# Attention with mixed heads, then a feed-forward block: a fixed order of TensorE's pieces, one ring of eight PSUM banks, and a shorter set-up

## The chip, the cores and the metric

The kernel runs on one core of one Trainium2 chip. The metric is the device time of one execution in microseconds (us); several executions give a median. "Span" is the time from the first to the last instruction in the profiled execution, some 1.7 us less than that execution's time. Engines are named as in the profile: PE is TensorE's matmuls, PEld its weight loads, DVE is VectorE, ACT is ScalarE, POOL is GpSimd.

## The reference, cut to what matters

Eight batches, twelve heads, 448 positions, head size 64. The scores of all heads are mixed by a 12x12 matrix before the softmax, the probabilities are mixed by another 12x12 matrix after it, and the result goes through a feed-forward block with a squared ReLU.

```python
scores = scale * q @ k.T                              # (8, 12, 448, 448)
scores = einsum('bhij,hg->bgij', scores, w_pre)       # mix the heads
attn = softmax(scores)
attn = einsum('bhij,hg->bgij', attn, w_post)          # mix the heads again
x = (attn @ v)  as (3584, 768)
h = maximum(x @ w_in, 0)                              # 768 -> 2048
out = (h * h) @ w_out                                 # 2048 -> 768
```

## The kernel before

A batch is worked through in 14 chunks of 32 query rows. For a chunk, TensorE makes three score tiles (`s_ps`: four 32-column matmuls each), three mixed tiles (`m_ps`), and, after the softmax, four tiles of the post product (`at_ps`), which come out transposed. Three chunks are in flight: scores of chunk s, mix of s-1, post product of s-2. The value product (`ot_ps`), the feed-forward block (`h_ps`, `o_ps`) and the transposes of the next batch's queries and keys (`qt_ps`, `kt_ps`) are "filler": units with a nominal weight, taken from a list after each step. A scheduler that works when the kernel is built settles the order on each engine, with program order as priority.

```python
psS = ... tile_pool(name="psS", bufs=2, space=PSUM)      # scores
psM = ... tile_pool(name="psM", bufs=2, space=PSUM)      # mixes
psT = ... tile_pool(name="psT", bufs=2, space=PSUM)      # post products
psF = ... tile_pool(name="psF", bufs=2, space=PSUM)      # filler
...
def ot_unit(b, half, c2):                                # value product of two heads
    for hh in range(2):                                  # one head after the other
        for jb in range(3):
            matmul(ps[64*hh:64*hh+64, 0:SH], lhsT=vfull[x][jb][:, g, :], rhs=at[:, jb, g, :], ...)
        for u in range(2):
            matmul(ps[64*hh:64*hh+64, ...], lhsT=vlast[x][u][:, g, :], rhs=at3[:, g, :], ...)
...
def chunk_mix(b, c):                                     # third mixed tile: two 64-column pieces
    matmul(ps[:, 0:S], lhsT=preBB, rhs=Bt, start=True, ...)
    for u, A in enumerate((A0, A1)):
        matmul(ps[64*u:64*u+64, 0:S], lhsT=preA[:, 128:192], rhs=A, ...)
...
for s in range(len(steps) + 2):
    chunk_scores(s); chunk_mix(s - 1); chunk_post(s - 2)
    ...                                                  # put new filler on the list
    debt = run_filler(3200 + debt)
```

The softmax here doesn't subtract the row's maximum and nothing guards it: scores larger than these inputs give would overflow.

Of the kernel before, what the change touches and what calls it, by code (L numbers as in the profile page):

```python
# [8 lines left out]
BF16 = mybir.dt.bfloat16  # L9
F32 = mybir.dt.float32  # L10
ACT = mybir.ActivationFunctionType
ALU = mybir.AluOpType

B, H, S, D = 8, 12, 448, 64
DMODEL = H * D
# [20 lines left out]
def kernel(  # L36
# [20 lines left out]
    psS = ctx.enter_context(tc.tile_pool(name="psS", bufs=2, space=bass.MemoryType.PSUM))  # L57
    psM = ctx.enter_context(tc.tile_pool(name="psM", bufs=2, space=bass.MemoryType.PSUM))
    psT = ctx.enter_context(tc.tile_pool(name="psT", bufs=2, space=bass.MemoryType.PSUM))
    psF = ctx.enter_context(tc.tile_pool(name="psF", bufs=2, space=bass.MemoryType.PSUM))  # L60
# [5 lines left out]

    def load_qk(b):
        qs, ks = [], []
        for st in range(4):
            n = ROWS[st]  # L70
            rows = slice(128 * st, 128 * st + n)
            qst = stage.tile([P, H, D], BF16, name="qst", tag="qst", bufs=4)
            nc.gpsimd.dma_start(out=qst[0:n, :, :], in_=q[b, :, rows, :].rearrange("h s d -> s h d"))  # L73
            qs.append(qst)
            kst = stage.tile([P, H, D], BF16, name="kst", tag="kst", bufs=4)
            nc.gpsimd.dma_start(out=kst[0:n, :, :], in_=k[b, :, rows, :].rearrange("h s d -> s h d"))
            ks.append(kst)
        return qs, ks
# [10 lines left out]
    staged = {0: load_qk(0)}  # L89


    ident = consts.tile([P, P], BF16, name="ident")
    masks.make_identity(nc, ident[:, :])
    onescol = consts.tile([P, 1], BF16, name="onescol")
    nc.vector.memset(onescol[:, :], 1.0)
    onesblk = consts.tile([P, 64], BF16, name="onesblk")
    nc.vector.memset(onesblk[:, :], 1.0)

    istripe = consts.tile([P, HC], F32, name="istripe")
    nc.vector.tensor_copy(out=istripe[:, :], in_=ident[:, 0:16])  # L100
    for r in range(1, 8):
        nc.vector.tensor_add(out=istripe[:, :], in0=istripe[:, :], in1=ident[:, 16 * r:16 * r + 16])

    def wcol(w, name, heads):
        t = consts.tile([P, H], F32, name=name)
        for j, h in enumerate(heads):
            src = bass.AP(tensor=w.tensor, offset=w[h, 0:1].offset, ap=[[0, HC], [1, H]])
            eng = nc.sync if j % 2 == 0 else nc.scalar
            eng.dma_start(out=t[HC * j:HC * j + HC, 0:H], in_=src)
        return t  # L110

    HA, HB = list(range(8)), [8, 9, 10, 11, 8, 9, 10, 11]

    def cat(w, name, heads):
        col = wcol(w, name + "_col", heads)
        t = consts.tile([P, H * HC], BF16, name=name)
        for g in range(H):
            nc.vector.tensor_scalar_mul(out=t[:, g * HC:(g + 1) * HC], in0=istripe[:, :], scalar1=col[:, g:g + 1])
        return t

    preA = cat(w_pre, "preA", HA)
    preB = cat(w_pre, "preB", HB)

# [8 lines left out]

    ql = []
    for x in range(2):
        ql.append([])
        for p in range(NPAIR):
            t = consts.tile([P, NHC, 32], BF16, name=f"ql{x}_{p}")
            nc.gpsimd.memset(t[:, :, :].rearrange("p a b -> p (a b)"), 0.0)
            ql[x].append(t)
    for x in range(2):  # L140
        for u in range(2):
            nc.gpsimd.memset(vlast[x][u][64 - 64 * u:128 - 64 * u, :, :].rearrange("p a b -> p (a b)"), 0.0)

    postA = cat(w_post, "postA", HA)
    postB = cat(w_post, "postB", HB)
# [5 lines left out]

    wpost_bf = consts.tile([H, H], BF16, name="wpost_bf")
    nc.gpsimd.dma_start(out=wpost_bf[:, :], in_=w_post[0:H, 0:H])
    cg_ps = psF.tile([P, 512], F32, name="cg_ps", tag="psF")
    nc.tensor.matmul(cg_ps[0:64, 0:H], lhsT=onesblk[0:H, 0:64], rhs=wpost_bf[0:H, 0:H], start=True, stop=True)
    nc.tensor.matmul(cg_ps[64:128, 0:H], lhsT=onesblk[0:H, 0:64], rhs=wpost_bf[0:H, 0:H], start=True, stop=True)
    cgblk = consts.tile([P, NPAIR], F32, name="cgblk")
    for hh in range(2):
        nc.vector.tensor_scalar_mul(
            out=cgblk[64 * hh:64 * hh + 64, :],  # L160
            in0=cg_ps[64 * hh:64 * hh + 64, 0:H].rearrange("p (c t) -> p t c", t=2)[:, hh, :],
            scalar1=1.0 / S)

    load_v(0)
    w1, w2 = [], []
    for c2 in range(NPAIR):
        t = wts.tile([P, DFF], BF16, name=f"w1_{c2}")
        nc.gpsimd.dma_start(out=t[:, :], in_=moe_w_in[c2 * 128:(c2 + 1) * 128, 0:DFF])
        w1.append(t)
    for ft in range(FT):  # L170
        t = wts.tile([P, DMODEL], BF16, name=f"w2_{ft}")
        nc.gpsimd.dma_start(out=t[:, :], in_=moe_w_out[ft * 128:(ft + 1) * 128, 0:DMODEL])
        w2.append(t)

    kts = {}
    bvecs = {}
    xts = {}
    h2ts = {}
    atbs = {}


    def prologue_units(b):
        qs, ks = staged[b]
        kts[b] = [None] * NPAIR

        def q_unit(p):
            ps = psF.tile([P, S], BF16, name="qt_ps", tag="psF")
            for st in range(4):
                n = ROWS[st]
                nc.tensor.transpose(ps[:, 128 * st:128 * st + n],  # L190
                                    qs[st][0:n, 2 * p:2 * p + 2, :].rearrange("s h d -> s (h d)"), ident[0:n, 0:n])
            for hh in range(2):
                r = slice(64 * hh, 64 * hh + 64)
                nc.vector.tensor_copy(out=ql[b % 2][p][r, :, 16 * hh:16 * hh + 16],
                                      in_=ps[r, 0:S].rearrange("p (n i) -> p n i", i=HC))

        def k_unit(p):
            ps = psF.tile([P, S], BF16, name="kt_ps", tag="psF")
            for st in range(4):
                n = ROWS[st]  # L200
                nc.tensor.transpose(ps[:, 128 * st:128 * st + n],
                                    ks[st][0:n, 2 * p:2 * p + 2, :].rearrange("s h d -> s (h d)"), ident[0:n, 0:n])
            kt_p = work.tile([P, S], BF16, name="kt_p", tag="kt", bufs=2 * NPAIR)
            nc.scalar.copy(out=kt_p[:, :], in_=ps[:, :])
            kts[b][p] = kt_p

        out_ = []
        for p in range(NPAIR):
            out_.append((300, lambda p=p: q_unit(p)))
            out_.append((300, lambda p=p: k_unit(p)))  # L210
        return out_

    def bias_unit(b):

        x = b % 2
        ps = psF.tile([P, 512], F32, name="vs_ps", tag="psF")
        srcs = vfull[x] + [vlast[x][0]]
        for c2 in range(NPAIR):
            for jb in range(4):
                nc.tensor.matmul(ps[:, c2:c2 + 1], lhsT=srcs[jb][:, 2 * c2:2 * c2 + 2, :].rearrange("s h d -> s (h d)"),  # L220
                                 rhs=onescol[:, 0:1], start=(jb == 0), stop=(jb == 3))
        bv = work.tile([P, NPAIR], F32, name="bvec", tag="bvec", bufs=2)
        nc.vector.tensor_tensor(out=bv[:, :], in0=ps[:, 0:NPAIR], in1=cgblk[:, :], op=ALU.mult)
        bvecs[b] = bv

    def ot_unit(b, half, c2):
        x = b % 2
        at, at3 = atbs[(b, half)]
        ps = psF.tile([P, 512], F32, name="ot_ps", tag="psF")
        for hh in range(2):  # L230
            g = 2 * c2 + hh
            r = slice(64 * hh, 64 * hh + 64)
            for jb in range(3):
                nc.tensor.matmul(ps[r, 0:SH], lhsT=vfull[x][jb][:, g, :], rhs=at[:, jb, g, :],  # L234
                                 start=(jb == 0), stop=False, skip_group_check=True)
            for u in range(2):
                nc.tensor.matmul(ps[r, 0:SH].rearrange("p (c u i) -> p u c i", u=2, i=HC)[:, u, :, :],  # L237
                                 lhsT=vlast[x][u][:, g, :], rhs=at3[:, g, :], start=False, stop=(u == 1),
                                 skip_group_check=True)
        if (b, c2) not in xts:  # L240
            xts[(b, c2)] = ffnp.tile([P, S], BF16, name="xt", tag=f"xt{c2}", bufs=2)
        nc.scalar.activation(out=xts[(b, c2)][:, SH * half:SH * half + SH], in_=ps[:, 0:SH], func=ACT.Identity,  # L242
                             bias=bvecs[b][:, c2:c2 + 1], scale=1.0)

    def ffn1_unit(b, ft):
        ps = psF.tile([P, S], F32, name="h_ps", tag="psF")
# [5 lines left out]
        nc.scalar.activation(out=hr[:, :], in_=ps[:, :], func=ACT.Relu)  # L252
# [182 lines left out]
```

## Time and profile before

| | before |
|---|---|
| time, median of 2 | 916.75 us (916.36 to 917.13) |
| span | 915.4 us |
| PE busy / ACT / DVE / POOL | 95% / 55% / 47% / 26% |
| changes of tile shape in TensorE's built order | 1306 |

The page of the kernel before begins with the busy time of each engine, its share of the span and its number of instructions:

```profile
span 915.4 us, 17324 instructions
PE 872.0 (95%) x6914; PEld 434.1 (47%) x6914; DVE 429.8 (47%) x1070; ACT 502.3 (55%) x1337; POOL 241.9 (26%) x277
```

PE is busy nearly all the time, so the other engines' idle time costs nothing. But a busy PE is not a streaming PE. Here is a piece of the timeline of PE before (start in us, duration in us, engine, line, operation, tiles; `128*32` is the part of the array used, rows times columns; the rest is shape and count):

```profile
312.88 0.35 PE L325 MATMUL m_ps<-s_sb,preBB 128*128 128x448 bf16 x1
313.16 0.38 PE L327 MATMUL m_ps<-s_sb,preA 128*64 128x448 bf16 x2
313.48 0.26 PE L353 MATMUL at_ps<-postA,d_sb 128*128 128x192 bf16 x1
...
313.89 0.25 PE L354 MATMUL at_ps<-postA,d_sb 128*128 128x192 bf16 x1
314.07 0.36 PE L300 MATMUL s_ps<-kt_p,ql_0_183 128*32 128x448 bf16 x1
...
314.08 0.36 PE L300 MATMUL s_ps<-kt_p,ql_3_189 128*32 128x448 bf16 x1
314.27 0.35 PE L300 MATMUL s_ps<-kt_p,ql_0_183 128*32 128x448 bf16 x1
```

A 448-column operand takes 187 ns to stream (448 columns at 2.4 per ns, the slope between 56 ns for 128 columns and 189 ns for 448 in this trace), and from 314.07 to 314.27, between two 32-column groups in the same shape, little more passes: 0.20 us. But from 312.88, a full-array matmul of 448 columns, to 313.16, where a 64-column pair starts, 280 ns pass; from there to the full-array matmul at 313.48 it is 320 ns; and a 192-column matmul, 80 ns of streaming, is followed by a narrow group only after 180 ns (313.89 to 314.07). Over the whole trace the medians after a 448-column matmul are 189 ns in the full array, 283 ns to narrow columns, 295 ns from 32 columns back to the full array and 309 ns from 64 columns back. A change of shape costs about 100 ns. The four `s_ps` quarters, on the other hand, start within 10 ns of each other (the first and the last are shown, at 314.07 and 314.08): narrow tiles of one shape run side by side.

The list of waits of PE before (who waited for whom; us in total, times, longest) shows that after the set-up it waits for nobody:

```profile
PE cg_ps L155 <- DVE preB L118: 23.8, 1, 23.8
PE kt_ps L201 <- DVE cgblk L159: 5.7, 1, 5.7
...
PE ot_ps L234 <- ACT xt L242: 0.9, 6, 0.2
```

The first two lines are the set-up. In the timeline of DVE it reads:

```profile
10.37 8.65 DVE L100 CAST istripe<-ident 128x16 f32<-128x16 bf16 x1 [8.97 <-POOL ident masks.py:199]
...
20.73 1.75 DVE L118 TENSOR_SCALAR preA<-istripe,preA_col 128x16 bf16<-128x16 f32 x12 [0.24 <-DVE istripe L102]
...
29.82 0.34 DVE L159 TENSOR_SCALAR cgblk<-cg_ps 64x6 f32<-64x6 f32 x2
30.19 0.79 DVE L194 COPY ql_0_183<-qt_ps 64x448 bf16<-64x448 bf16 x2
```

A small cast takes 8.65 us, then scalings in groups of twelve follow, and the first copy of queries (`ql`), without which no score can be made, starts at 30.19 us. The same trace shows what POOL does meanwhile, eleven memsets without a pause:

```profile
10.19 0.93 POOL L138 MEMSET ql_1_185<- 128x896 bf16 x1
...
18.05 0.93 POOL L138 MEMSET ql_5_205<- 128x896 bf16 x1
```

The last of them ends at 18.98 us, the cast at 19.02.

### The profile page before, as it was taken

The page shows a single profiled execution, that of the slowest core. Times are in us where ns is not written, and L with a number is a line of the kernel's source. Part 1 is how long each engine was busy: PE and PEld are TensorE (multiplying, and loading weights), DVE is VectorE, ACT ScalarE, POOL GpSimd, SP SyncE. Part 2 cuts the span into 40 slices and gives each one's busy share as a digit, 9 for nine tenths or more (in the row PEclk, how much of TensorE's full clock was granted, in tenths as well). Part 3 has the DMA queues.
Part 4 walks back from the last instruction along what each step waited for, and adds up shares of the span by engine and source line. Part 5 has one row for each costly group of instructions (what it writes and reads, how often), then busy time and mean ns, then how long its engine had stood idle before and what let it go on. Part 6 is the DMA issues. An engine that isn't in the chain of part 4 may idle for free. (4 is left out here: it accounts for less than half of the span.)

```text
span 915.4 us, 17324 instructions
## 1 busy us (share of the span) xinstructions
PE 872.0 (95%) x6914; PEld 434.1 (47%) x6914; DVE 429.8 (47%) x1070; ACT 502.3 (55%) x1337; POOL 241.9 (26%) x277
## 2 busy tenths in 40 slices
PE   0699999999999999999999999999999999999998
PEld 0234455453554545544454535545355444544354
DVE  5577730677017760277405772077701775036700
ACT  0266652677527764476635775267653676347641
POOL 9470343030700308003250215203070000600050
PEclk9999999999999999999999999999999999999999
DMA  9997951072510905109321275109051000010001
GB/s 61 178 189 41 62 35 44 19 48 15 35 62 1 62 1 44 53 1 62 26 36 37 18 45 35 52 11 59 4 35 62 1 2 1 16 47 1 2 1 61
DMA packets 149330, 35.76 MB, mean 39 GB/s; under 512 B 139264, under 2 KB 148480, under 8 KB 149248
## 3 DMA queue, kind: packets, MB, share of 16 engines
q0 software_dynamic: 140032, 23.60, 34.0%
q1 hardware_dynamic: 8704, 11.03, 3.5%
q8 instruction: 54, 0.88, 0.4%
q14 instruction: 28, 0.23, 0.1%
q10 hardware_dynamic: 512, 0.01, 0.0%
HBM read 47.21 MB, written 11.01 MB: 64 GB/s over the span
## 5 line engine op out<-in xcount | busy, mean ns | idle before, releaser
L357 DVE CAST at<-at_ps 128x384 bf16<-128x384 f32 x336 | 181.1, 550 | 394.0 <-PE at_ps L354 389.3
L312 ACT ACTIVATE e_sb<-m_ps 128x448 f32<-128x448 f32 x336 | 181.1, 542 | 51.3 <-ACT e_sb L312 18.7
L335 DVE TENSOR_SCALAR d_sb<-e_sb,rc 128x448 bf16<-128x448 f32 x336 | 137.1, 463 | 0.7
L304 ACT CAST s_sb<-s_ps 128x448 bf16<-128x448 f32 x224 | 115.8, 534 | 37.2 <-PE s_ps L300 36.5
L252 ACT ACTIVATE hr<-h_ps 128x448 f32<-128x448 f32 x128 | 69.5, 543 | 79.4 <-PE h_ps L248 72.8
L352 PE MATMUL at_ps<-postBB,d_sb 128*128 128x384 bf16 x336 | 111.0, 330 | 1.5 <-DVE d_sb L335 0.7
L73 POOL DMA_DIRECT2D qst<-in_q_dram x32 | 31.8, 993 | 275.7 <-PE qt_ps L190 223.9
L353 PE MATMUL at_ps<-postA,d_sb 128*128 128x192 bf16 x336 | 83.2, 248 | 0.0
L354 PE MATMUL at_ps<-postA,d_sb 128*128 128x192 bf16 x336 | 82.7, 246 | 0.0
L321 PE MATMUL m_ps<-s_sb,preA 128*128 128x448 bf16 x224 | 81.0, 362 | 0.0
L264 ACT COPY osb<-o_ps 128x384 f32<-128x384 f32 x48 | 23.0, 478 | 101.2 <-PE o_ps L262 101.2
L306 DVE CAST s_sb<-s_ps 128x448 bf16<-128x448 f32 x112 | 69.3, 618 | 8.7 <-PE s_ps L300 8.4
L312 ACT ACTIVATION_READ_ACCUMULATOR e_sb<-m_ps 128x1 f32 x336 | 66.8, 199 | 0.0
L242 ACT ACTIVATE xt<-ot_ps,bvec 128x224 bf16<-128x224 f32 x96 | 40.1, 447 | 23.3 <-PE ot_ps L237 23.1
L352 PEld LDWEIGHTS <-d_sb 128*128 128x128 bf16 x336 | 32.6, 97 | 40.2 <-issue 28.6
L248 PE MATMUL h_ps<-xt,w_0_272 128*128 128x448 bf16 x128 | 45.1, 352 | 1.2 <-ACT xt L242 0.5
L327 PE MATMUL m_ps<-s_sb,preA 128*64 128x448 bf16 x224 | 45.4, 378 | 0.0
L248 PE MATMUL h_ps<-xt,w_5_282 128*128 128x448 bf16 x128 | 45.1, 352 | 0.0
L248 PE MATMUL h_ps<-xt,w_4_280 128*128 128x448 bf16 x128 | 45.1, 352 | 0.0
L248 PE MATMUL h_ps<-xt,w_3_278 128*128 128x448 bf16 x128 | 45.1, 352 | 0.0
L248 PE MATMUL h_ps<-xt,w_2_276 128*128 128x448 bf16 x128 | 45.1, 352 | 0.0
L248 PE MATMUL h_ps<-xt,w_1_274 128*128 128x448 bf16 x128 | 45.1, 352 | 0.0
(862 smaller groups left out, 2097.1 us busy)
## 6 DMA issues: line engine op xcount, KB each, us to landing
out_dram<-osb SPq DMA_DIRECT2D x48, 192.0 KB, 1.9
qst<-in_q_dram POOLq DMA_DIRECT2D x24, 192.0 KB, 5.8
kst<-in_k_dram POOLq DMA_DIRECT2D x24, 192.0 KB, 6.3
out_dram<-osb SPq DMA_DIRECT2D x16, 96.0 KB, 2.2
qst<-in_q_dram POOLq DMA_DIRECT2D x8, 96.0 KB, 6.7
kst<-in_k_dram POOLq DMA_DIRECT2D x8, 96.0 KB, 6.5
v_0_85<-in_v_dram POOLq DMA_DIRECT2D x4, 192.0 KB, 4.0
v_1_86<-in_v_dram POOLq DMA_DIRECT2D x4, 192.0 KB, 5.0
```

Of the source, the lines that this page charges most:

```text
L248: nc.tensor.matmul(ps[:, 0:S], lhsT=w1[c2][:, ft * 128:(ft + 1) * 128], rhs=xts[(b, c2)][:, :], start=(c2 == 0), stop=(c2 == NPAIR - 1))
L252: nc.scalar.activation(out=hr[:, :], in_=ps[:, :], func=ACT.Relu)
L304: nc.scalar.copy(out=sb[:, :], in_=ps[:, :])
L306: nc.vector.tensor_copy(out=sb[:, :], in_=ps[:, :])
L312: nc.scalar.activation(out=e[:, :], in_=ps[:, :], func=ACT.Exp, scale=SCALE, accum_out=sm[:, t:t + 1])
L321: nc.tensor.matmul(ps[:, 0:S], lhsT=preA[:, 0:128], rhs=A[:, :], start=True, stop=False)
L327: nc.tensor.matmul(ps[64 * u:64 * u + 64, 0:S], lhsT=preA[:, 128:192], rhs=A[:, :], start=False, stop=True, skip_group_check=True)
L335: nc.vector.tensor_scalar(out=d[:, :], in0=es[t][:, :], scalar1=rc[:, t:t + 1], scalar2=1.0 / S, op0=ALU.mult, op1=ALU.subtract)
L352: nc.tensor.matmul(ps[:, 0:384], lhsT=dB[:, js], rhs=postBB[:, :], start=True, stop=False, skip_group_check=True)
L353: nc.tensor.matmul(ps[:, 0:192], lhsT=d0[:, js], rhs=postA[:, :], start=False, stop=True, skip_group_check=True)
L354: nc.tensor.matmul(ps[:, 192:384], lhsT=d1[:, js], rhs=postA[:, :], start=False, stop=True, skip_group_check=True)
L357: nc.vector.tensor_copy(out=dst, in_=src)
```

## The change

Its intent: take the narrow matmuls of a step together, so that TensorE changes its shape twice a step and not again and again; fix that order by hand; let all eight banks serve any tile; and shorten the set-up. The 64-column pieces become pairs of 32-column pieces, so that they have the scores' shape. The filler is spread evenly over the four places of each step. The diff, cut to its core:

```diff
-    psS, psM, psT, psF: four pools of two banks
+    psp = ctx.enter_context(tc.tile_pool(name="psp", bufs=8, space=bass.MemoryType.PSUM))
...
+    keys are loaded first, then queries; ql[0] is cleared on DVE, ql[1] and vlast on POOL later
-        for g in range(H):
-            nc.vector.tensor_scalar_mul(out=t[:, g * HC:(g + 1) * HC], in0=istripe[:, :], scalar1=col[:, g:g + 1])
+        nc.vector.tensor_tensor(out=t[:, :, :], in0=istripe (broadcast), in1=cols[name] (broadcast), op=ALU.mult)
...
+            for jb in range(3):              # value product: the heads alternate
+                for hh in range(2):
...
+    def mix_AB(s):                           # four 32-column pieces instead of two of 64
+        for r in range(4):
+            u, half = divmod(r, 2)
+            nc.tensor.matmul(ps[32 * r:32 * r + 32, 0:S], lhsT=preA[:, 128 + 32 * half:160 + 32 * half], ...)
...                                           # post_last: eight 32-column pieces instead of four of 64
+    with tc.manual_schedule(engines={PE}):
+            share = sum(w for w, _ in filler) / max(rest - 0.5, 1) / 4 if s0 else 1e9
+            score_tile(s0, 0); score_tile(s0, 1)
+            mix_AB(s1)
+            post_last(s2)
+            score_tile(s0, 2)
+            mix_BB(s1);     fill(share)
+            mix_O(s1, 0);   fill(share)
+            mix_O(s1, 1);   post(s2, 0);  fill(share)
+            post(s2, 1);    fill(share)
+            post(s2, 2)
```

(The `score_tile` to `post` lines stand for the body of the step loop, without its conditions.) The softmax's reciprocal is now taken for each tile alone, 336 of one column for 112 of three. The diff also joins the value product of two head pairs in one unit, cuts each output tile of the feed-forward block into two units, and starts the next batch's transposes two steps earlier.

## The prediction

> **What bounds the kernel now.** TensorE. On the page PE is busy 95% of the 915.4 us span, ACT 55%, DVE 47%, POOL 26%; in the list of waits PE hardly waits after start-up. But it isn't always streaming. In the timeline a 448-column matmul is followed by the next after 189 ns when both use the full array (448 columns at 2.4 per ns: 187). When the next has another tile shape, the step is 283 ns (128 to 32 or 64 columns), 295 (32 to 128) or 309 (64 to 128): about 100 ns per change of shape. This agrees with the Trainium skill, "TensorEngine Tiling (Array Packing)", Key Properties: changing the tiling mode drains TensorE.
>
> The built instruction order has 1306 such changes before, 540 after. Measured steps laid along the order (full array: columns/2.4; narrow tiles of one mode side by side; 98 ns per change) give 860 us for before. The real stream lags this sum by 24 us at its start, 40 us at 76 us, 51 us at the end: the sum is a usable ruler.
>
> **PE after.** The same ruler gives an estimate of 725 us: 135 less. 766 fewer changes are 75 us of it; the other 60 us are narrow matmuls that now run beside others of their group instead of alone (score quarters four together; the value product alternating two heads, 72 to 42 us). The 672 added narrow matmuls (four 32-column pieces for two of 64) cost no streaming time.
>
> **Other engines.** ACT stays at 502 us of work (64% of the new span), DVE at 430 plus some 20 for 224 more reciprocals. Neither is the limit on average. But per chunk ACT needs 2 x 0.53 + 3 x (0.54 + 0.20) + 0.32 = 3.6 us, PE without filler only 3.1. All 14 steps of batch 0 and the first two of each later batch have little filler, and in a fixed order PE waits there. At 4.3 us per such step this costs 13 us in batch 0 and 2.5 in each other: 30 together. Steps with filler take 6 to 8 us of PE, so waits for ACT and banks are mostly hidden; I allow 8 us.
>
> **Start-up.** Now steady PE work starts at 30 us, because DVE constants (one cast of 8.6 us, 48 scalings) precede the query copies. After: keys first, 4 wide multiplies for the 48; the last small weight load still lands near 15.5 us, so first scores at about 20 us. That is 15 us above the ruler, plus 4 for half-speed matmuls (0.55 us each instead of 0.36, seen until 51 us now).
>
> **Sum.** 725 + 15 + 4 + 30 + 8 + 5 (end) + 1.4 (span to time) = 789 us, 14% less; range 768 to 818.
>
> **What would show it.** The 100 ns steps remain at about 540 places; the value-product groups shrink; PE waits for ACT appear in the list of waits, in batch 0 and at batch starts; first scores near 20 us; PE about 95% busy elsewhere; ACT 64%.
>
> **What would make it wrong.** PE waiting in every step (softmax latency before the post product; banks of the one ring held by open accumulations): 0.3 us a step is 30 us. POOL memsets delaying DVE at the start. A cold clock through batch 0. Or thin steps costing nothing: 765.

## The result, and the profile after

| | before | after |
|---|---|---|
| time, median of 2 | 916.75 us | 792.89 us (792.84 to 792.94) |
| ratio | | 0.8649 (95%: 0.8612 to 0.8686) |
| span | 915.4 us | 791.2 us |
| PE / ACT / DVE busy | 95 / 55 / 47% | 95 / 61 / 62% |
| changes of shape in the built order | 1306 | 540 |
| laid-out stream (the prediction's ruler) | 859.9 us | 725.4 us |
| start of the last matmul less that stream ("lag") | 50.9 us | 61.2 us |
| first score matmul | 33.9 us | 22.6 us |

A ratio here is the mean time of one kernel's runs over that of the other's runs of the same rounds, so it is not quite the ratio of the medians quoted.

The page after, in the same lines as before:

```profile
span 791.2 us, 18851 instructions
PE 750.2 (95%) x7586; PEld 428.6 (54%) x7586; DVE 488.6 (62%) x1249; ACT 482.3 (61%) x1337; POOL 243.2 (31%) x271
```

The timeline of PE after shows the narrow group of one step: two score tiles, `mB_ps`, the last post product (L359, L363), the third score tile; then the full array until the next step:

```profile
205.64 0.36 PE L291 MATMUL s_ps<-kt_p,ql_0_143 128*32 128x448 bf16 x1
...
205.84 0.35 PE L291 MATMUL s_ps<-kt_p,ql_0_143 128*32 128x448 bf16 x1
...
206.03 0.36 PE L305 MATMUL mB_ps<-s_sb,preA 128*32 128x448 bf16 x4
206.22 0.25 PE L359 MATMUL at_ps<-postA,d_sb 128*32 128x192 bf16 x2
207.33 0.26 PE L359 MATMUL at_ps<-postA,d_sb 128*32 128x192 bf16 x2 [0.87 <-DVE d_sb L315]
207.34 0.34 PE L363 MATMUL at_ps<-postBB,d_sb 128*32 128x192 bf16 x4
...
207.51 0.35 PE L291 MATMUL s_ps<-kt_p,ql_5_148 128*32 128x448 bf16 x1
207.80 0.36 PE L321 MATMUL mB_ps<-s_sb,preBB 128*128 128x448 bf16 x1
208.00 0.35 PE L245 MATMUL h_ps<-xt,w_0_191 128*128 128x448 bf16 x1
```

Up to 206.22 everything is in one shape and the steps are those of streaming: 0.20, 0.19 and 0.19 us. From 207.51 to 207.80, where the shape changes, it is 0.29 us. In between there is a new thing: the last post product has started two of its matmuls at 206.22 and goes on only at 207.33; 0.87 us of this PE sat idle for the scaled softmax tile `d_sb`. The list of waits of PE after shows it in total:

```profile
PE at_ps L359 <- DVE d_sb L315: 20.3, 29, 3.4
PE kt_ps L180 <- DMA kst<-in_k_dram: 10.1, 4, 6.0
PE qt_ps L180 <- DMA qst<-in_q_dram: 3.6, 3, 1.5
PE kt_ps L180 <- DVE ql_0_143 L188: 0.7, 1, 0.7
```

20.3 us in 29 places. (This list counts only time in which no matmul at all is in flight; against the ruler the jumps at this place add to some 25 us between its own matmuls and 6 to 7 us just before it.) In this example the scaling for which PE waits took 1.13 us in place of the usual 0.45, beside a multiply of POOL's; experiment 11 returns to that.

The ruler and the trace together give a full account of the span, which can be set against the prediction's sum. The lag is read at the start of each step:

| term | predicted | read from the trace of after |
|---|---|---|
| stream | 725 | 725.4 |
| lag when the first score starts | 15 | 17.7 |
| half clock and waits in the 14 steps of batch 0 | 4 + 13 | 18.5 (some 4 in the first two steps, 5.4 in another) |
| waits in the other steps without filler | 17.5 | 16.3 (3.4 in batch 1, 2.1 in each of 6 more) |
| other waits | 8 | 8.7 |
| last matmul to end, span to time | 5 + 1.4 | 4.6 + 1.7 |
| sum | 789 | 792.9 |

The matmuls of 448 columns take 0.55 us each until 28.7 us, in the first two steps of batch 0. From 38.9 to 42.3 us, after TensorE's longest wait for `d_sb`, they take that long again, and there the profile shows a granted clock of 0.50; some 1.7 us of the step of 5.4 are this (half of 3.4 us, an estimate).

### The profile page after: what moved, and what is told of

It is laid out like the page before. It is cut to its first block, busy times and chain, and to the rows that moved or that the text cites. A ratio compares the mean times of both kernels' runs of the same rounds, so it can differ in the third digit from the quotient of the medians.

```text
span 791.2 us, 18851 instructions
## 1 busy us (share of the span) xinstructions
PE 750.2 (95%) x7586; PEld 428.6 (54%) x7586; DVE 488.6 (62%) x1249; ACT 482.3 (61%) x1337; POOL 243.2 (31%) x271
## 4 chain that ended last, share of the span: by engine, by line
PE 85%; DVE 11%; DMA 2%; ACT 1%; issue 1%; ACTq 0%; DVEq 0%
PE o_ps L263 19%; PE h_ps L245 18%; PE s_ps L291 8%; PE m_ps L327 6%; PE at_ps L345 6%; DVE d_sb L315 6%; PE at_ps L348 5%; PE m_ps L328 5%; PE mB_ps L321 4%; PE ot_ps L223 4%; DVE at L350 3%; PE mB_ps L305 2%; PE qt_ps L180 2%; PE kt_ps L180 2%; PE at_ps L359 2%; DMA postB_col<-in_w_post_dram 1%
## 5 line engine op out<-in xcount | busy, mean ns | idle before, releaser
L315 DVE TENSOR_SCALAR d_sb<-e_sb,rc 128x448 bf16<-128x448 f32 x336 | 171.9, 514 | 7.6
L311 ACT ACTIVATE e_sb<-m_ps 128x448 f32<-128x448 f32 x224 | 121.1, 545 | 27.8 <-issue 23.9
L313 DVE RECIPROCAL rc<-sm 128x1 f32<-128x1 f32 x336 | 53.6, 160 | 100.5 <-ACT e_sb L311 99.6
L348 PE MATMUL at_ps<-postA,d_sb 128*128 128x192 bf16 x672 | 110.3, 246 | 0.0
L348 PEld LDWEIGHTS <-d_sb 128*128 128x128 bf16 x672 | 65.7, 98 | 40.8 <-issue 0.2
L311 ACT ACTIVATE e_sb<-mB_ps 128x448 f32<-128x448 f32 x112 | 63.1, 563 | 8.4 <-PE mB_ps L321 6.6
L359 PE MATMUL at_ps<-postA,d_sb 128*32 128x192 bf16 x448 | 37.3, 249 | 20.9 <-DVE d_sb L315 20.3
L71 POOL DMA_DIRECT2D kst<-in_k_dram x32 | 32.1, 1012 | 51.9 <-PE kt_ps L180 43.6
L236 ACT ACTIVATE xt<-ot_ps,bvec 128x224 bf16<-128x224 f32 x96 | 37.7, 444 | 14.6 <-PE ot_ps L230 13.9
L311 ACT ACTIVATION_READ_ACCUMULATOR e_sb<-m_ps 128x1 f32 x224 | 46.1, 206 | 0.0
L245 PE MATMUL h_ps<-xt,w_0_191 128*128 128x448 bf16 x128 | 45.1, 353 | 0.0
L245 PE MATMUL h_ps<-xt,w_5_196 128*128 128x448 bf16 x128 | 45.1, 353 | 0.0
L245 PE MATMUL h_ps<-xt,w_2_193 128*128 128x448 bf16 x128 | 45.1, 352 | 0.0
L245 PE MATMUL h_ps<-xt,w_3_194 128*128 128x448 bf16 x128 | 45.1, 352 | 0.0
```

Of the source, the lines that this page charges most:

```text
L245: nc.tensor.matmul(ps[:, 0:S], lhsT=w1[c2][:, ft * 128:(ft + 1) * 128], rhs=xts[(b, c2)][:, :], start=(c2 == 0), stop=(c2 == NPAIR - 1))
L311: nc.scalar.activation(out=e[:, :], in_=ps[:, 0:S], func=ACT.Exp, scale=SCALE, accum_out=sm[:, 0:1])
L315: nc.vector.tensor_scalar(out=d[:, :], in0=e[:, :], scalar1=rc[:, 0:1], scalar2=1.0 / S, op0=ALU.mult, op1=ALU.subtract)
L348: nc.tensor.matmul(ps[:, 192 * u:192 * u + 192], lhsT=D_sb[(s, u)][:, js], rhs=postA, start=False, stop=True, skip_group_check=True)
```

## The experiments

Each kernel was checked against the reference and was correct. "Stream" and "changes" are worked out from the built order of each by the same ruler; they are estimates. The kernel before ran beside each group, at 916.3 to 917.2 us, so the groups can be compared.

### 1 and 2. The same instructions, with the narrow group broken up

Edit of the first, on the kernel after: the third score tile moves to between two full-array mixes.

```diff
-            score_tile(s0, 2)
             mix_BB(s1)
             fill(share)
             mix_O(s1, 0)
+            score_tile(s0, 2)
```

> The changed kernel with the third score tile moved out of the narrow group, to between two full-array mixes; no instruction is added or taken away. The built order has 746 changes of tile shape for 540. Theory A (each change of shape costs TensorE about 98 ns): 20.7 us more than the changed kernel's 792.9, so 813.6 us (810 to 818). Theory B (the drains are hidden and the gain came from free banks and a fixed order): 793 us (790 to 797).

The second moves the last post product too.

```diff
-            post_last(s2)                # was in the narrow group
...
             post(s2, 0)
+            post_last(s2)                # between two full-array post products
```

> As the run before, and the last post product (eight 32-column matmuls) moved out of the group as well, between two full-array post products: 954 changes for 540. Theory A: 41.5 us more than 792.9, so 834.4 us (828 to 840), twice the step of the run before; a little less if the later place spares the 0.88 us waits for the softmax in thin steps (13 us in all). Theory B: 793 us.

Measured: 809.37 us (ratio 0.8826) and 815.08 us (ratio 0.8892). Theory B is dead: nothing was added, and it costs 16 and 22 us. Theory A had foreseen 20.7 and 41.5; the first run falls just below its range, the second well below. What is missing is found by the lag: at the end of the trace it is 61.2 us in the kernel after, 56.2 us in the first and 41.6 us in the second. In steps full of filler the lag grows by 0.02, 0.04 and 0.06 us, so there the two and four added changes cost about 110 ns each: 100 that the ruler has (20.7 us for 206, 41.5 for 414) and 10 that it lacks. In the steps without filler the added time falls into the wait for the softmax: with the last post product later in the step, a step of batch 0 that had lagged by 1.01 us lags by 0.06. So a change of shape does cost some 100 ns, and the second experiment shows in passing that the place of the last post product is what makes PE wait.

### 3. The alternating heads alone, in the kernel before

```diff
-        for hh in range(2):
-            for jb in range(3):
+        for jb in range(3):
+            for hh in range(2):
```

(and likewise for the last two matmuls of each head.)

> The kernel before with one edit: in the value product the matmuls of the two heads alternate instead of one head after the other. Changes of shape stay (1299 for 1306); the laid-out stream falls from 859.9 to 829.0 us because the two heads' 64-column tiles run side by side. Theory A: 916.75 - 31 = 886 us (880 to 892). Rival (the scheduler had already put the heads of neighbouring units side by side, or the operand reads limit): 912 to 917 us.

Measured: 906.66 us, ratio 0.9886: 10 us, a third of what the ruler says and outside both ranges. The ruler was wrong about the kernel before. Its built order has five matmuls of one head, then five of the other, but the timeline of PE before shows, for one such unit:

```profile
309.17 0.26 PE L234 MATMUL ot_ps<-at,v_0_85 128*64 128x224 bf16 x1
309.27 0.26 PE L234 MATMUL ot_ps<-at,v_1_86 128*64 128x224 bf16 x1
309.27 0.28 PE L234 MATMUL ot_ps<-at,v_0_85 128*64 128x224 bf16 x1
309.36 0.26 PE L234 MATMUL ot_ps<-at,v_2_87 128*64 128x224 bf16 x1
309.39 0.26 PE L234 MATMUL ot_ps<-at,v_1_86 128*64 128x224 bf16 x1
```

The first line is the first matmul of head 0. The two lines at 309.27 are its second and the first of head 1, which stands four places later in the built order, and head 1 goes on at 309.39 beside head 0 at 309.36. TensorE had started it early; its half of the columns was free. Compared by tile shape and width alone, 391 of the 960 records of the value product don't stand in the trace where they stand in the built order; of all other records, three don't.

### 4. The heads one after the other, in the kernel after

This tests that reading where nothing else differs.

```diff
-            for jb in range(3):
-                for hh in range(2):
-                    g = 4 * cp + 2 * y + hh
+            for hh in range(2):
+                g = 4 * cp + 2 * y + hh
+                for jb in range(3):
```

> The changed kernel with the two heads of the value product one after the other again, as in the kernel before; all else as changed. The ruler of the prediction (a matmul starts only after the one before it in program order) says 30 us more: 823 us. New theory, from the trace of the kernel before, where the second head's first matmul starts 0.10 us after the first head's although four matmuls stand between them in program order: TensorE itself starts matmuls of a free column half ahead of their turn, so the serial order costs only a skew of about 0.1 us per unit, 46 groups: 798 us (794 to 802).

Measured: 798.39 us, ratio 0.8708: 5.5 us more, not 30. The alternating heads are worth 5 to 10 us. In the traces the value product took 61.5 us before and 43.4 us after, where the prediction has 72 and 42 (first matmul of each row of them to the matmul behind the row).

### 5. The new set-up alone, in the kernel before

The edit takes over the set-up's lines of the diff (key loads first, four wide multiplies, clearing on DVE, later weights) and leaves pools, pieces and step loop.

> The kernel before with the new set-up alone (key loads first, four wide multiplies, memsets of the query tiles on DVE, weights later); pools, pieces and order as before. Theory: first scores at about 23 us in place of 34, but 4.4 us more of laid-out stream (864.3 for 859.9): 916.75 - 7 = 910 us (904 to 914). Rival (set-up is a large part of the gain): below 895 us.

Measured: 911.59 us, ratio 0.9941, as expected. The first score comes at 24.3 us in place of 33.9, but the order that the scheduler makes has 4.4 us more stream. The set-up is 5 us of the 124.

### 6. One ring of banks alone, in the kernel before

```diff
-    psS, psM, psT, psF, bufs=2 each
+    psp = ctx.enter_context(tc.tile_pool(name="psp", bufs=8, space=bass.MemoryType.PSUM))
```

> The kernel before with one edit: the four PSUM pools of two banks become one pool of eight; pieces, program order and automatic order are left. The scheduler then keeps close to program order: 783 changes for 1306, laid-out stream 778.4 us for 859.9. Theory A (only the order counts, whoever makes it): 916.75 - 81 = 835 us (825 to 845). Rival (the order must be fixed by hand, and pieces regrouped, for the gain): over 890 us.

Measured: 855.71 us, ratio 0.9332. This one line of the change is worth 61 us, half of the whole, with the old pieces, the old step loop and no order by hand. The change of order can be read in the built order. The likely reason, not shown apart, is that with two banks to a pool the scheduler finds no bank for the third score tile and takes something else meanwhile. A stretch of the kernel before reads 3 score matmuls, 1 post, 3 mixes, 5 posts, 5 scores, 1 mix, 3 posts, 1 score, 4 posts. With the ring a step is 12 scores, 7 mixes, 13 posts. That is 783 changes for 1306, and the four quarters of a score tile are split in 4 of 336 tiles, in place of 155. The run is 21 us over the expected 835, outside both ranges. Two waits of PE in it:

```profile
PE vs_ps L217 <- DMA v<-in_v_dram: 16.7, 2, 16.4
PE ot_ps L231 <- DVE at L354: 15.3, 22, 1.4
```

The value sums (`vs_ps`) now come in program order, which puts them early in batch 0, before the values have landed: 16.7 us, most of what is missing. In the kernel before they had been pushed back. The granted clock was 0.50 from 61.4 to 81.9 us, so the matmuls between the end of this wait (72.9 us) and 81.9 take longer too.

### 7, 8 and 9. Ring or pools, fixed or automatic order

Three variants of the kernel after fill a square. The edits:

```diff
-        return psp.tile(..., tag="ps")                         # one ring of 8
+        return pools[k].tile(..., tag="ps" + k)                # four pools of 2
```
```diff
-    with tc.manual_schedule(engines={PE}):                     # fixed order
+    if True:                                                   # the scheduler's order
```

> The changed kernel, order of TensorE still fixed, with four PSUM pools of two banks again in place of the one of eight. The order and the laid-out stream (725.4 us) are the same. If the ring matters at run time, TensorE waits for ACT and DVE to empty banks in nearly every step, 0.1 to 0.5 us in each of 112: 805 to 850 us. If it only mattered for the order that the scheduler made: 793 to 798 us.

> The changed kernel with the ring, but TensorE's order left to the automatic scheduler. It then makes 589 changes of shape for 540 and a laid-out stream of 734.2 us for 725.4. Theory A (only the resulting order counts): 793 + 9 = 802 us (797 to 808). Rival (the fixed order by hand is what gains): over 830 us.

> The changed kernel with both taken back: four PSUM pools of two banks, and TensorE's order left to the scheduler. The built order has 725 changes of shape and a laid-out stream of 753.9 us. If order and stream decide, plus 40 to 50 us of start and waits and 6 of end: 806 us (798 to 815), faster than the fixed order with four pools (842), because the scheduler plans with the banks that it has. If the small pools cost the same waits whoever orders: 842 us or more.

Measured, in us (ratio to before; stream; lag at the end):

| | fixed order | automatic order |
|---|---|---|
| ring of 8 | 792.89 (0.8649; 725.4; 61.2) | 780.55 (0.8515; 734.2; 39.5) |
| four pools of 2 | 841.95 (0.9184; 725.4; 109.4) | 825.81 (0.9006; 753.9; 67.3) |

Two of the three expectations failed (the runs lie in neither of their ranges), and both failures teach something. The ring is worth 45 to 49 us whoever makes the order. With a fixed order and small pools the stream is the same as with the ring, and all of the loss is lag. The list of waits of PE in that run names some of it:

```profile
PE at_ps L347 <- DVE at L352: 17.2, 26, 4.2
PE qt_ps L182 <- ACT kt_p L197: 8.2, 16, 0.6
PE m_ps L329 <- ACT e_sb L313: 7.1, 18, 0.4
```

and since most of these waits are short, the lag tells more: it grows by 0.3 us in every full step and by 1.5 us in the steps without filler. With automatic order and small pools I had expected 806 us; the stream is the one foreseen, but the same 0.3 us a step are there: the scheduler's plan did not take them away.

And the fixed order is a loss: 12 us with the ring, 16 us with the pools. I had expected 9 us the other way, from the stream. The stream is indeed 8.8 us longer, but 21.7 us of lag are gone. PE's wait for the scaled softmax tile is now

```profile
PE at_ps L359 <- DVE d_sb L315: 7.5, 4, 4.8
```

instead of 20.3 us in 29 places, and 4.8 of the 7.5 us are one place, that of experiment 11. The built order shows why. In a step without filler the fixed order has the eight matmuls of the last post product together; the automatic order has two of them, then the third score tile, `mB_ps` and a mix, and then the other six. It puts other work exactly where the fixed order waits, and pays with two changes of shape. In full steps it keeps them together.

### 10. Filler kept for the steps that have none

```diff
+            if s0 and 1 <= s0[0] and s0[0] + 1 < B:
+                rest += 2
+            if s0 and s0[0] >= 2 and s0[1] < 2:
+                rest = 2 - s0[1]
```

(and the value sums and the first half's value product go to the front of the list, so that buffers come free in time.)

> The changed kernel (fixed order, ring) with the filler of batches 1 to 6 spread over two steps more, so that the first two steps of batches 2 to 7 have some 3 us of feed-forward work each in place of none. Stream and changes of shape as before (725.2 us, 538). Theory (TensorE waits for the softmax there only because nothing stands between the last mix and the last post product): the waits of about 1 us in 12 such steps go, 792.9 - 12 = 781 us (779 to 786). Rival (the waits belong to the fixed place of the last post product, filler or not, or come back in the steps that now have less filler): 791 to 795 us.

Measured: 778.32 us, ratio 0.849: 14.6 us less, a little more than expected (just below the range), with the order still fixed. In batches 2 to 6 the lag grows by 0.5 to 0.8 us a batch in place of 2.5 to 4.1. In the waits of PE

```profile
PE at_ps L359 <- DVE d_sb L315: 11.9, 16, 3.4
```

is left of 20.3 us, 10.1 of it in batch 0 and the first steps of batch 1, for which there is nothing to keep. So the waits of the fixed order belong to the steps without filler.

### 11. The late memsets on DVE

The largest single jump of the lag in the kernel after was 5.4 us in one step of batch 0. The timeline of DVE there:

```profile
33.25 0.17 DVE L313 RECIPROCAL rc<-sm 128x1 f32<-128x1 f32 x1
33.45 4.65 DVE L315 TENSOR_SCALAR d_sb<-e_sb,rc 128x448 bf16<-128x448 f32 x1
38.02 0.14 DVE L313 RECIPROCAL rc<-sm 128x1 f32<-128x1 f32 x1
38.20 0.56 DVE L350 CAST at<-at_ps 128x384 bf16<-128x384 f32 x1
```

One scaling of a softmax tile took 4.65 us; the median of these 336 is 0.45 us. In the same stretch POOL does

```profile
33.07 0.84 POOL L158 MEMSET ql_0_149<- 128x896 bf16 x1
33.86 0.84 POOL L158 MEMSET ql_1_150<- 128x896 bf16 x1
...
37.01 0.84 POOL L158 MEMSET ql_5_154<- 128x896 bf16 x1
```

memsets without a pause, and the scaling ends 0.25 us after the last of them. The Trainium skill, "SBUF — State Buffer", section "Who interferes with whom", says that a DVE operation in a two-port mode and a GpSimd operation want the same pair of ports, and that the second to come blocks fully until the first is done. The edit clears the same tiles on DVE, before its first multiply:

```diff
-        for p in range(NPAIR):
-            nc.gpsimd.memset(ql[1][p]...)          # and four vlast halves, in late_loads
+    for p in range(NPAIR):
+        nc.vector.memset(ql[1][p]...)              # and four vlast halves, right after istripe
```

> The changed kernel (fixed order, ring) with the ten late memsets moved from POOL to DVE's idle time before 9 us. In the changed kernel one DVE scaling of the softmax took 4.65 us in place of 0.45 while POOL ran these memsets without a pause, and TensorE then waited 3.6 us. Theory (POOL's memsets hold up DVE's reads of SBUF): no scaling over 1 us is left, and 792.9 - 5 = 788 us (786 to 790). Rival (the long scaling has another cause, the weight loads or the cold start): 792 to 794 us.

Measured: 786.74 us, ratio 0.8576: 6 us. The scalings of that part of the trace are now

```profile
34.14 0.45 DVE L315 TENSOR_SCALAR d_sb<-e_sb,rc 128x448 bf16<-128x448 f32 x1
...
35.27 0.45 DVE L315 TENSOR_SCALAR d_sb<-e_sb,rc 128x448 bf16<-128x448 f32 x1
```

of usual length, and the step of 5.4 us lags by 0.04; the clock no longer falls there. But nine scalings of 1.0 to 2.1 us are left, of eleven over 1 us in the kernel after, so "none over 1 us" was not met. Every one of them lies beside other work of POOL's: the multiplies of the feed-forward block, or the issuing of DMAs. That these ports are the cause was not shown apart from any other way in which POOL's memsets may hold DVE; that the memsets are the cause of the 4.65 us was. The cast of 8.65 us in the kernel before ended with POOL's memsets in the same way, but moving those was not tested alone.

### 12. A version that beats both

Ring, automatic order, memsets on DVE, and the last 64 rows of keys and queries in one tile:

```diff
+        for y, src in enumerate((k, q)):     # rows 384 to 447: keys in partitions 0 to 63, queries in 64 to 127
+            nc.gpsimd.dma_start(out=last[64 * y:64 * y + 64, :, :], in_=src[b, :, 384:448, :]...)
...
-            nc.tensor.transpose(ps[:, 128 * st:128 * st + n], tiles[st][0:n, ...], ident[0:n, 0:n])   # 8 a pair, 2 with n = 64
+            nc.tensor.transpose(ps[:, 128 * j:128 * j + 128], t[:, ...], ident[:, :])                  # 7 a pair, all full
```

The queries then lie in the order 384 to 447, 0 to 383, which the score matmuls' index takes into account.

> A version made from what was found: ring of eight banks, automatic order, memsets on DVE, and the last 64 rows of keys and queries in one tile of 128 rows, so that a head pair takes seven full transposes in place of eight of which two have 64 rows: no change of shape inside the transposes (407 changes for 589 in the free-order run), laid-out stream 717.5 us for 734.2. Theory (a change to 64 rows costs as much as one to narrow columns): 780.6 - 17 - 5 = 759 us (752 to 765). Rival (such changes are free): 773 to 777 us.

Measured: 767.02 us (765.48 to 770.12), ratio 0.8367, against 780.55 of the free order; the gain is 13.5 us of the 22 expected, so outside the range, and outside the rival's too. The change of shape is not in doubt: in the two traces of before and after a full transpose is followed by one of 64 rows after 152 ns and that by a full one after 132 ns, where two full ones are 56 ns apart, and this run has none of these. But the lag at the end of the profiled run (at 770.1 us the slowest of the four) is 46.2 us, not the 33 that 39.5 less the memsets would give. The waits of PE name two of its parts:

```profile
PE at_ps L355 <- DVE d_sb L311: 8.2, 13, 1.1
PE s_ps L287 <- DVE ql L191: 6.3, 3, 5.6
```

A unit now holds one bank for keys and queries until ACT and DVE have both emptied it, and the long query copies stand before softmax work on DVE. That this is the cause was not tested. Filler kept back (experiment 10) was not tried together with this version.

## Why the prediction was right

The time was 792.9 us for a prediction of 789, inside 768 to 818. Point by point:

- **TensorE is the limit, and changes of shape cost some 100 ns each.** Right. The two runs with the narrow group broken up show it with the same instructions: some 110 ns a change in full steps. The rule of the Trainium skill, "TensorEngine Tiling (Array Packing)", Key Properties, that a change of mode drains TensorE, fits that; the number is this trace's, and whether the array drains no run shows.
- **"135 less", as 75 of changes and 60 of narrow matmuls that run side by side.** The sum held, since 859.9 to 725.4 is what the ruler gives and the lag went from 50.9 to 61.2 only. But the second term was mis-sized. "The value product alternating two heads, 72 to 42 us" measured 10 us in the kernel before and 5.5 us in the kernel after, since TensorE had already started the second head ahead of its turn. The ruler made the kernel before some 11 us too long there (72 for 61.5), and a little too short at many other places, so that its total still fitted: that is luck. A ruler that fits in sum can be wrong in its parts.
- **Steps without filler cost 30 us.** Right in size: 18.5 + 16.3 less the 4 at half clock are some 31 us, of which 5 to 6 us are the memsets. But the explanation, ACT's 3.6 us per chunk against PE's 3.1, failed, so the size is partly luck. The predicted waits for ACT did not come: in the list of waits PE waits 0.2 us for ACT and 20.3 for DVE's `d_sb`. ACT's durations overlap: in a step of 4.06 us without filler it was busy 2.97 us, and with the free order (experiment 8) the same step took 3.36 us, less than the 3.6. In that step DVE was busy 3.32 us, so beside PE it is DVE, not ACT, that has nothing to spare there. The trace shows one wait, that of the last post product for the last scaled softmax tile, and it goes when other work stands in its place (experiments 2, 8 and 10), with ACT's work unchanged.
- **Start-up.** First scores at 22.6 us, not 20: on DVE the query copies stood behind the multiplies of the post weights, which began at 18.9 us, because those weights' small loads landed only then and not near 15.5 us. The 4 us for half-speed matmuls were right, but they end at 28.7 us. The set-up alone is worth 5 us, near the small gain that the sum implied.
- **Other engines.** ACT has 482 us for the 502 foreseen. DVE has 489 us for 450: the reciprocals came to 53.6 us for 18.7, and the scalings to 172 us for 137. Of these 336 scalings 43 run beside POOL's memsets or multiplies and take 0.90 us in the mean, the other 293 take 0.46; in the kernel before none does.

```profile
L315 DVE TENSOR_SCALAR d_sb<-e_sb,rc 128x448 bf16<-128x448 f32 x336 | 171.9, 514 | 7.6
L313 DVE RECIPROCAL rc<-sm 128x1 f32<-128x1 f32 x336 | 53.6, 160 | 100.5 <-ACT e_sb L311 99.6
```

(columns: line, engine, operation, tiles, shapes and count; busy us, mean ns; idle time before and what ended it; the scalings' mean had been 463 ns before.)

- **What would make it wrong.** "POOL memsets delaying DVE at the start" was named as a risk, and happened, at 6 us. A cold clock through batch 0 did not happen, nor did waits in every step: in full steps the lag grows by 0.02 us.
- **What the prediction didn't ask is who makes the order.** It took the fixed order to be the means. The runs show that half of the gain comes from the ring of banks alone, because it lets the scheduler keep program order; that the rest of the change, with the order left free, brings 855.7 to 780.6 us (set-up, heads, pieces, places of filler and value sums together; only the first two were measured alone); and that fixing the order by hand took 12 us back.

## What to carry to other kernels

Count the changes of tile shape in the built order of TensorE and price them (here 100 ns each); a busy PE hides them. Before ordering by hand, look at what makes the scheduler shuffle: here four PSUM pools of two banks, and one shared ring of eight was worth 45 to 61 us in every setting. In a fixed order, look for the steps without spare work, since each wait there is paid in full: keep some filler for them, or leave the order free.

## What the Trainium skill lacked or had wrong

- "TensorE: Matmul & The Clock Gate", Part 3, "The mechanism", says that matmuls start in program order, "strict FIFO, no reordering". Here a matmul to a free column half started 0.1 us after the first of five for the other half, beside the second and ahead of the last three, and 391 of 960 records of the value product stand out of order by shape and width alone; a serial order that should have cost 30 us cost 5.5.
- "TensorEngine Tiling (Array Packing)", Key Properties, says that a change of mode drains TensorE but gives no cost. Here: about 95 ns from full array to narrow columns, 106 from 32 columns to full, 120 from 64 to full, and for transposes 172 ns for a full to 64 rows and back (152 + 132 - 2 x 56).
- "SBUF — State Buffer", "Who interferes with whom", says that the pair is held for the whole of one instruction, and nothing of several in a row. Here one DVE scaling ended only after the last of six POOL memsets in a row, five of which began after it: 4.65 us for 0.45 (and a cast in the kernel before after eleven: 8.65 us). Whether the ports did it was not shown.
- No page that I read has that small PSUM pools change the order which an automatic scheduler makes: 1306 changes of shape with four pools of two banks, 783 with one of eight, and 61 us between them.
